# Attention bursts of a four-layer kernel: scores and values as one operation per query block, strips between eights, and a new order

## The chip, the cores and the metric

The kernel runs on one core of a Trainium2 chip. The metric is the time of one execution on the device in microseconds (us), as the median of several runs. The core has five engines with a queue of instructions each: TensorE (PE in the profile, with its weight loads as PEld), VectorE (DVE), ScalarE (ACT), GpSimd (POOL) and SyncE (SP, which here issues nearly all transfers). An engine works through its queue in order and waits at semaphores for the others.

## The reference

The input x has 2048 rows of 448 numbers (bf16). Four layers follow each other, each added to x: attention, gated MLP, attention, gated MLP, with the same weights in both rounds.

```
x = x + A(layernorm(x));  x = x + B(layernorm(x));  x = x + A(layernorm(x));  x = x + B(layernorm(x))

A: qkv = x @ wqkv, 16 heads of 28; row s attends to the rows s, s-2, s-4, ... s-14 (8 of them, those below 0 masked)
   o = softmax(q.k * 28**-0.5) @ v;  return o @ wo
B: return ((x @ w_gate) * (x @ w_up)) @ w_down      (448 -> 1792 -> 448)
```

## The kernel before

**Tiling.** Everything stays in on-chip memory; weights and x are loaded once. Layer norm is done by VectorE and ScalarE per block of 128 rows, and the result is transposed, by TensorE in the head and by transfers later. All large products (L349) are made as pairs: the contraction is cut into pieces of 64 rows, and two products of 64x128 tiles run side by side on the upper and lower half of the array. Such an operation is a "twin" (L652, L665): two outputs A and B, where the upper half works first on A and the lower on B, and then they cross over. At the crossing TensorE waits on its own semaphore until the other half's results are written.

**Attention.** The 2048 rows are cut into 17 query blocks (the first of 128, the others of 120 rows), taken as nine groups: block 0 alone, then pairs. For a group, `attn_front` (L812) makes the masked copies of q (`Qz`, L821, VectorE), the scores (L835, TensorE), the exponential in two halves (L844, ScalarE) and the minimum with a mask (L851, VectorE), also in halves. `attn_back` (L855) multiplies by the values (L869, TensorE), copies the result out of PSUM (L880, L884), and `norm` (L889) divides by the row sums (L894 to L907). Then `y_blocks` makes the out-projection.

The scores and values of a group are 64 small products each (32 for block 0, fewer and wider in the first layer's first six groups, `WIDE_S`). They use tiles of 64x32, eight of which work at once, and so stand as a burst between the whole products of 64x128. The scores of one group are one operation that takes four PSUM banks (`Banks(4)`). Its exponentials wait for all of them. The values of a group are one operation too, which waits for both halves of the exponentials and minima (L872).

**Strips.** A whole product can also be given as four strips of 64x32 (L351, recorded at L352), which use the burst's own tiles. A pair is then eight strips. An operation that lends its first steps as strips is the host of the burst.

**The order.** Operations are recorded in Python (`sc.add`) and get numbers. Which engine does an operation and in which order is a written list, `ORDER` (L102), and the PSUM banks come from another, `BANKS` (L163). An entry of TensorE's list such as `406*2/397` means: operation 406 (a burst), cut at k = 2 points, with the first two steps of 397 as strips at the cuts, and then the rest of 397. The cuts stand at equal shares (L242): 64 products become 21, 21 and 22 with two strip steps, four times 16 with three. At most three steps can be lent (`MAXALT`, L31), and only the first ones of a host. All waits of a burst and of its host are put ahead of the first of their instructions (L312 to L325).

Of the kernel before, what the change touches and what calls it, by code (L numbers as in the profile page):

```python
# [7 lines left out]
S = 2048  # L8
# [20 lines left out]
BURST = "C32"  # L29
WIDE_S = ((0, 0), (0, 1), (0, 2), (0, 3), (0, 4), (0, 5))  # L30
MAXALT = 3  # L31
# [63 lines left out]
def grp_nc(g):  # L95
# [21 lines left out]
    ),  # L117
    "act": (
# [12 lines left out]
    ),  # L131
    "dve": (
# [46 lines left out]
)  # L179


# [924 lines left out]
```

## Time and profile before

| | |
|---|---|
| Three runs | 387.46, 387.26, 386.85 us (median 387.26) |
| Span of the profiled execution | 386.8 us, the only time shown for it |
| Whole products (L349), 512 columns, for gate and up | 1146, 376 ns each as recorded |
| Products of the values (L869), 64 columns | 1024, 192 ns each as recorded |
| Products of the scores (L835), 64x32 tiles | 736, 191 or 199 ns each as recorded |
| Strips (L352) of WD, 448 columns | 216, 354 ns each as recorded |
| Weight loads (PEld) | 215.7 us busy, beside the products |

The granted clock of TensorE is 1.000 over the whole span. A product's recorded time holds its way through the array, and several are on their way at once, so the times of products can't be added: the distance between their starts tells what one costs. In the timeline a row is a run of equal products: start in us, time from the first's start to the last's end, engine, line, names, shapes and count. Because the ends overlap, the next row's start can stand ahead of the row's end.

### The profile page before, as it was taken

To read this page: it belongs to the slowest core of one execution; us is meant where nothing else is said; L and a number is where in the kernel's file an instruction comes from. 1 tells how busy PE (TensorE), PEld (TensorE's weight loads), DVE (VectorE), ACT (ScalarE), POOL (GpSimd) and SP (SyncE) were. 2 spreads that over 40 slices of the span, in tenths; PEclk is the share of its full clock that TensorE was granted. 3 is DMA by queue.
4 is the path that set the end of the run, shared out by engine and by line. 5 is a ranking of instruction groups with operands and counts; after the bars stand their busy time and mean duration, and the time that the engine had idled before them with its cause. 6 is when DMAs were issued, how large, how long until landed. Compare 5 with 4: busy or idle time off the path is not lost. (4 is left out here: it accounts for less than half of the span.)

```text
span 386.8 us, 14289 instructions
## 1 busy us (share of the span) xinstructions
PE 378.7 (98%) x6326; PEld 215.7 (56%) x6326; DVE 286.9 (74%) x644; ACT 204.3 (53%) x391; POOL 7.2 (2%) x33
## 2 busy tenths in 40 slices
PE   8999998999999999999999999999999999999997
PEld 3654576644554445555865666555555444445775
DVE  7988899998947887696776886578886887562423
ACT  5997886764516564364466426637653834143220
POOL 7000000000000000000000000000000000000000
PEclk9999999999999999999999999999999999999999
DMA  7665541801313041141104115400142005020004
GB/s 259 159 160 148 103 116 55 103 18 24 66 32 44 3 83 34 32 53 28 29 3 64 29 15 98 67 16 2 24 73 51 2 2 97 25 47 2 26 2 132
DMA packets 54881, 22.50 MB, mean 58 GB/s; under 512 B 45012, under 2 KB 54820, under 8 KB 54820
## 3 DMA queue, kind: packets, MB, share of 16 engines
q1 hardware_dynamic: 54676, 21.53, 27.5%
q8 instruction: 50, 0.82, 0.9%
q14 instruction: 11, 0.09, 0.1%
q10 hardware_dynamic: 144, 0.06, 0.1%
HBM read 8.54 MB, written 2.71 MB: 29 GB/s over the span
## 5 line engine op out<-in xcount | busy, mean ns | idle before, releaser
L349 PE MATMUL ps<-xnTb,WGU 64*128 64x512 bf16 (+1 forms) x1930 | 177.2, 333 | 0.9 <-issue 0.9
L349 PEld LDWEIGHTS ps<-xnTb,WGU 64*128 64x128 bf16 x1930 | 95.4, 94 | 73.2 <-issue 3.1
L960 ACT ACTIVATE g_sb<-ps 128x512 bf16<-128x512 f32 (+1 forms) x140 | 69.1, 511 | 91.3 <-PE ps L349 79.6
L963 DVE TENSOR_TENSOR hT<-g_sb,ps 128x512 bf16<-128x512 bf16 (+1 forms) x140 | 78.0, 574 | 39.9 <-ACT g_sb L960 36.7
L349 PE MATMUL ps<-WD,hT 64*128 64x448 bf16 x786 | 82.0, 349 | 0.1
L349 PEld LDWEIGHTS ps<-WD,hT 64*128 64x128 bf16 x786 | 38.9, 94 | 32.2 <-issue 1.0
L924 DVE TENSOR_TENSOR x_sb<-x_sb,ps 128x448 bf16<-128x448 bf16 x62 | 36.9, 614 | 26.1 <-PE ps L349 26.1
L349 PE MATMUL ps<-xnTa,WQK 64*128 64x512 bf16 (+1 forms) x486 | 52.2, 353 | 0.7 <-DVE xnTa L625 0.6
L844 ACT ACTIVATE E_sb<-ps,shift_sb 128x1024 bf16<-128x1024 f32 (+1 forms) x36 | 37.3, 1067 | 13.1 <-PE ps L835 13.1
L580 DVE BATCH_NORM_STATS2 st<-x_sb 128x6 f32<-128x448 bf16 x64 | 38.6, 615 | 1.5 <-DMA x_sb<-in_A_x_dram 1.2
L601 DVE TENSOR_SCALAR xn_sb<-x_sb,mv,rstd 128x896 bf16<-128x896 bf16 (+1 forms) x64 | 35.6, 573 | 4.4 <-ACT rstd L585 4.3
L349 PEld LDWEIGHTS ps<-xnTa,WQK 64*128 64x128 bf16 x486 | 23.3, 94 | 21.5 <-DVE WQK L527 0.7
L710 ACT ACTIVATE qk<-ps 128x1024 bf16<-128x1024 f32 (+1 forms) x29 | 26.2, 918 | 9.3 <-PE ps L349 9.2
L349 PE MATMUL ps<-wo_g,oT 64*128 64x448 bf16 x252 | 28.7, 349 | 0.2
L851 DVE TENSOR_TENSOR E_sb<-E_sb,MK 128x1024 bf16<-128x1024 bf16 (+1 forms) x36 | 23.3, 659 | 7.5 <-ACT E_sb L844 7.3
L895 ACT ACTIVATE R_sb<-R_sb 128x480 f32<-128x480 f32 (+1 forms) x34 | 20.4, 602 | 9.1 <-DVE R_sb L894 8.8
L907 DVE TENSOR_TENSOR oT<-O_sb,R_sb 128x480 bf16<-128x480 f32 (+3 forms) x36 | 22.0, 626 | 2.3 <-ACT R_sb L896 2.2
L349 PE MATMUL ps<-WV,xnTa 64*128 64x336 bf16 (+3 forms) x246 | 23.4, 304 | 0.1
L894 DVE STREAM_SHUFFLE R_sb<-O_sb 128x480 f32<-128x480 f32 (+1 forms) x34 | 23.2, 691 | 0.0
L583 ACT ACTIVATE lnv<-mv,eps_sb 128x2 f32<-128x2 f32 (+1 forms) x33 | 9.7, 292 | 22.7 <-DVE mv L582 22.6
L896 ACT ACTIVATE R_sb<-R_sb 128x480 f32<-128x480 f32 (+1 forms) x34 | 20.1, 601 | 0.4
L880 ACT ACTIVATE O_sb<-ps 128x512 f32<-128x512 f32 (+2 forms) x21 | 11.4, 567 | 12.9 <-PE ps L869 12.9
(65 smaller groups left out, 222.3 us busy)
## 6 DMA issues: line engine op xcount, KB each, us to landing
out_dram<-x_sb SPq DMA_DIRECT2D x15, 112.0 KB, 1.8
x_sb<-in_A_x_dram SPq DMA_DIRECT2D x3, 448.0 KB, 5.8
hT<-in_A_wqkv_dram SPq DMA_DIRECT2D x4, 224.0 KB, 4.5
WGU<-in_B_w_gate_dram SPq DMA_DIRECT2D x4, 224.0 KB, 3.5
WGU<-in_B_w_up_dram SPq DMA_DIRECT2D x4, 224.0 KB, 4.4
WD<-in_B_w_down_dram SPq DMA_DIRECT2D x2, 448.0 KB, 3.9
WGU<-in_B_w_gate_dram SPq DMA_DIRECT2D x2, 336.0 KB, 4.4
WGU<-in_B_w_up_dram SPq DMA_DIRECT2D x2, 336.0 KB, 4.5
```

The source lines that it names most:

```text
L349: return lambda E: E.matmul(out(), lhs(), rhs(), start=start, stop=stop)
L580: sc.add("dve", one(lambda E, B=B: E.bn_stats(st6[:, B, :], x_sb[:, B, :]), ("bn", li, B)), 525.0, deps=[("x", li - 1, B)] + ([("xn", li - ...
L601: sc.add("dve", one(lambda E, B=B, dst=dst, src=src: E.tensor_scalar(dst, src, mv[:, B, 0:1], rstd[:, B:B + 1], ALU.subtract, ALU.mult), ( ...
L710: return E.activation(dst, src, ACT.Copy) if hasattr(E, "activation") else E.tensor_copy(dst, src)
L844: return E.activation(E_sb[:, slot, 2 * hp:2 * hp + 2, 0:w], ps[:, b0:b0 + 2, 0:w], ACT.Exp, bias=shift_sb[:, 0:1], scale=SCALE)
L851: return E.tensor_tensor(e, e, MK[:, kind, 0:nc].unsqueeze(1).unsqueeze(1).to_broadcast([128, 2, w // nc, nc]), ALU.min)
L894: sc.add("dve", one(lambda E: E.stream_shuffle(R_sb[:, rs, 0:w], O_sb[:, os_, 0:w], [DH] * 32), ("Rs", li, qb)), dve_est(w) + 20.0, deps=[ ...
L895: sc.add("act", one(lambda E: E.activation(R_sb[:, rs, 0:w], R_sb[:, rs, 0:w], ACT.Ln), ("Rl", li, qb)), act_est(w, False), deps=[("Rs", l ...
L907: return E.tensor_tensor(oT[:, :, a % HALF:a % HALF + z - a], O[:, :, a - tok:z - tok], R_sb[:, rs, 0:w].rearrange("p (h n) -> p h n", h=4 ...
L924: sc.add("dve", one(lambda E: E.tensor_tensor(x_sb[:, B, :], x_sb[:, B, :], ps[:, bk[w], 0:D], ALU.add), ("x", li, B)), dve_est(D), deps=[ ...
L960: sc.add("act", one(lambda E, gs=gs, bk=bk: E.activation(g_sb[:, gs, 0:nt], ps[:, bk[0], 0:nt], ACT.Copy), ("G", li, j, fc)), act_est(nt), ...
L963: sc.add("dve", one(lambda E, gs=gs, bk=bk, fc=fc: E.tensor_tensor(hT[:, fc, hs, 0:nt], g_sb[:, gs, 0:nt], ps[:, bk[1], 0:nt], ALU.mult), ...
```

## The change

Scores and values are now two operations per group, one per half (for a pair of query blocks: one per block). Each half of the scores has a pair of PSUM banks of its own, and its exponential waits for that half alone. Each half of the values waits for its own half of the exponentials and for its own block's v. The copies out of PSUM wait for both.

Strips: every step of an operation can be lent, any number of steps, from any step on, and several hosts can share a burst: an entry such as `508/2/1` behind the star names the host, the number of steps and the first of them. The cuts are rounded to eight products (`cut_of`). An operation's waits are put ahead of its own first instruction, not ahead of the whole entry. `ORDER` and `BANKS` are new throughout: TensorE's products are the same in number and size but for strips (448 before, 400 after, the others back as whole products), and some copies out of PSUM change between ScalarE and VectorE.

```diff
-MAXALT = 3
...
-                    cut = [len(short) * (i + 1) // (k + 1) for i in range(k)] + [len(short)]
-                        if i < k:
-                            seq += [(host, fn) for fn in host.alt[i]]
-                    seq += [(host, n) for n in range(2 * k, len(host.ins))]
+                    hosts = [tuple(int(i) for i in (h + "/0").split("/")[:3]) for h in tail.split("+")]
+                    seq = [(self.ops[h], n, None) for h, k, f in hosts for n in range(2 * f)]
+                    sets = [[(self.ops[h], n, fn) for fn, n in self.ops[h].alt[f + i]] for h, k, f in hosts for i in range(k)]
+                    for i in range(len(sets) + 1):
+                        z = cut_of(len(short), i + 1, len(sets) + 1)
+                        seq += short[a:z] + (sets[i] if i < len(sets) else [])
...
+def cut_of(n, i, parts):
+    return n if i >= parts else min(n, (2 * n * i + 8 * parts) // (16 * parts) * 8)
...
-        bk = Banks(4, pair=True)
-        if li > 0 and g:
-            deps = deps + [("E", li, g - 1, 0), ("E", li, g - 1, 1)]
+        bks = [Banks(2, pair=True) for _ in range(2)]
...
+        for hp, ins in enumerate(parts):
+            ins[-1] = (ins[-1][0], [("Sh", li, g, hp)] + ([("S", li, qbs[hp])] if nd == 2 else [("S", li, qbs[0])] if hp else []))
+            first = sc.add("pe", ins, 0.0, deps=deps + [("Qz", li, g)], mode="C64" if wide else BURST, acquire=bks[hp], prio=prio, after=first)
...
-            sc.add("act", one(fe, ("Ex", li, g, hp)), act_est(2 * w), deps=[("S", li, qbs[-1]), prev, "c_shift"], release=[(bk, 2 * hp), (bk, 2 * hp + 1)], prio=prio)
+            sc.add("act", one(fe, ("Ex", li, g, hp)), act_est(2 * w), deps=[("Sh", li, g, hp), prev, "c_shift"], release=[(bks[hp], 0), (bks[hp], 1)], prio=prio)
...
-        sc.add("pe", ins, AV_EST * nd / 2, deps=[("E", li, g, 0), ("E", li, g, 1), "c_v"] + [(k, li, q) for k in ("V", "VT") for q in qbs] + [r[1] for r in oring], mode=BURST, acquire=bk, prio=prio)
+        for hp, ins in enumerate(parts):
+            ins[-1] = (ins[-1][0], [("Ah", li, g, hp)] + ([("AV", li, qbs[hp])] if nd == 2 else [("AV", li, qbs[0])] if hp else []))
+            first = sc.add("pe", ins, 0.0, deps=[("E", li, g, hp), "c_v"] + [(k, li, q) for k in ("V", "VT") for q in (qbs[hp:hp + 1] if nd == 2 else qbs)], mode=BURST,
+                           acquire=None if hp else bk, prio=prio, after=first)
...
-            sc.add(AVC_E, one(fo, ("Oc", li, g, c)), {"act": act_est(n), "dve": dve_est(n)}, deps=[("AV", li, qbs[0])] + [r[1] for r in oring],
+            sc.add(AVC_E, one(fo, ("Oc", li, g, c)), {"act": act_est(n), "dve": dve_est(n)}, deps=[("AV", li, qbs[-1])] + [r[1] for r in oring],
```

In the order that results, the bursts of 64x32 tiles stand as follows (products, with | for a strip step):

| | before | after |
|---|---|---|
| 32 without strips | 2 | 15 |
| 16 \| 16 | 0 | 3 |
| 64 without strips | 1 | 0 |
| 64 as 21 \| 21 \| 22 | 13 | 0 |
| 64 as 16 \| 16 \| 16 \| 16 | 6 | 5 |
| 64 as 24 \| 16 \| 24 | 0 | 3 |
| 64 as 40 \| 16 \| 8 or 8 \| 16 \| 40 | 0 | 4 |
| 64 as 16 \| 8 \| 16 \| 8 \| 16 | 0 | 2 |
| 96 (24 \| 24 \| 24 \| 24; 16 \| 16 \| 16 \| 48) | 1 | 1 |
| 128 (32 \| 32 \| 32 \| 32; none) | 2 | 1 |
| 64 values, then 64 scores as 16 \| 16 \| 16 \| 16 | 1 | 0 |
| 64 scores with seven steps in their first half, then 64 values | 0 | 1 |

The six bursts of wide scores (tiles of 64x64, first layer) are the same in both.

More of the change, by code (lines that the diff above doesn't have):

```diff
@@ L235, in schedule @@
                 w, _, tail = w.partition("*")
-                k, _, host = tail.partition("/")
                 got = [self.ops[int(i)] for i in w.split("+")]
-                seq = [(o, n) for o in got for n in range(len(o.ins))]
-                if k:
-                    short, k, host = seq, int(k), self.ops[int(host)]
-                    got.append(host)
-                    cut = [len(short) * (i + 1) // (k + 1) for i in range(k)] + [len(short)]
-                    seq, a = [], 0
-                    for i, z in enumerate(cut):
-                        seq += short[a:z]
+                seq = [(o, n, None) for o in got for n in range(len(o.ins))]
+                if tail:
+                    hosts = [tuple(int(i) for i in (h + "/0").split("/")[:3]) for h in tail.split("+")]
+                    short, a = seq, 0
+                    seq = [(self.ops[h], n, None) for h, k, f in hosts for n in range(2 * f)]
[3 more added lines that the diff above has]
+                        seq += short[a:z] + (sets[i] if i < len(sets) else [])
                         a = z
-                        if i < k:
-                            seq += [(host, fn) for fn in host.alt[i]]
-                    seq += [(host, n) for n in range(2 * k, len(host.ins))]
+                    for h, k, f in hosts:
+                        got.append(self.ops[h])
+                        seq += [(self.ops[h], n, None) for n in range(2 * (f + k), len(self.ops[h].ins))]
                 for o in got:
@@ L289, in emit @@
                     continue
-                for op, n in seq:
-                    if isinstance(n, int) and ((op.idx, n) in used or n == len(op.ins) - 1):
+                for op, n, _ in seq:
+                    if n is not None and ((op.idx, n) in used or n == len(op.ins) - 1):
                         count[e] += 1
@@ L311, in run @@
                 for got, seq in self.order[e]:
-                    waits = {}
-                    for op in got:
-                        for k in op.deps:
-                            src, n = self.ready[k]
+                    begun = set()
+                    for op, n, fn in seq:
+                        waits = {}
+                        for k in op.deps if op.idx not in begun else ():
+                            src, m = self.ready[k]
                             if src.dma is not None:
@@ L320, in run @@
                                     continue
-                                s, v = src.eng, value[(src.idx, n)]
+                                s, v = src.eng, value[(src.idx, m)]
                             waits[s] = max(waits.get(s, 0), v)
-                    for s, v in waits.items():
-                        if seen.get(s, 0) < v:
-                            E.wait_ge(sems[s], v)
-                            seen[s] = v
-                    for op, n in seq:
-                        if not isinstance(n, int):
-                            n(E)
-                            continue
-                        i = op.ins[n][0](E)
+                        begun.add(op.idx)
+                        for s, v in waits.items():
+                            if seen.get(s, 0) < v:
+                                E.wait_ge(sems[s], v)
+                                seen[s] = v
+                        i = (fn or op.ins[n][0])(E)
                         if op.dma is not None:
@@ L353, in pair, with alt_of @@
     ins = [(whole(*a[:5]), a[6]) for a in calls]
-    strips = [strip(*a[:6], c) for a in calls for c in range(0, 128, 32)] if all(a[6] is None for a in calls) else None
-    return ins, strips
-def alt_of(strips, keep=1):
-    n = 0
-    while n < len(strips) - keep and strips[n] is not None:
-        n += 1
-    return strips[:min(n, MAXALT)]
+    return ins, [(strip(*a[:6], c), w if c == 96 else None) for w, a in enumerate(calls) for c in range(0, 128, 32)]
+def alt_of(steps):
+    return [[(fn, None if w is None else 2 * i + w) for fn, w in step] for i, step in enumerate(steps)]
+def cut_of(n, i, parts):
+    return n if i >= parts else min(n, (2 * n * i + 8 * parts) // (16 * parts) * 8)
 def act_est(n, psum=True):
@@ L857, in attn_back @@
         nd = len(qbs)
-        bk = Banks(2, pair=True)
+        bk = Banks(2)
         while nd == 2 and rpos["o"] % NO == NO - 1:
@@ L861, in attn_back @@
         oring = [ring("o", ("N", li, q)) for q in qbs]
-        ins = []
+        parts = [[], []]
         for hc, d, c, b in [(hc, d, c, b) for hc in range(4) for d in range(nd) for c in range(2) for b in range(4)]:
@@ L868, in attn_back @@
             eo = (2 * eh + b % 2) * nc
[L869 removed]
+            parts[eb // 2].append((lambda E, b=b, c=c, o=o, vw=vw, eb=eb, eo=eo: E.matmul(ps[32 * b:32 * b + 32, bk[c], o:o + nc], vw, E_sb[64 * c:64 * c + 64, slot, eb, eo:eo + nc],
                                                                start=True, stop=True, tile_position=(64 * c, 32 * b)), None))
[L871 to L872 removed]
+        first = None
+        for hp, ins in enumerate(parts):
+            ins[-1] = (ins[-1][0], [("Ah", li, g, hp)] + ([("AV", li, qbs[hp])] if nd == 2 else [("AV", li, qbs[0])] if hp else []))
+            first = sc.add("pe", ins, 0.0, deps=[("E", li, g, hp), "c_v"] + [(k, li, q) for k in ("V", "VT") for q in (qbs[hp:hp + 1] if nd == 2 else qbs)], mode=BURST,
+                           acquire=None if hp else bk, prio=prio, after=first)
         o0, nq = oring[0][0], qb_info(qbs[0])[3]
```

14 lines of the change are left out of this document (5 added, 9 removed), and 127 rows, old and new, of tables (BANKS, ORDER).

## The prediction

> **What bounds the kernel now.** I read the page's busy times first, then the waits of TensorE, then the timeline of TensorE around each attention burst.
>
> ```profile
> span 386.8 us, 14289 instructions
> PE 378.7 (98%) x6326; PEld 215.7 (56%) x6326; DVE 286.9 (74%) x644; ACT 204.3 (53%) x391; POOL 7.2 (2%) x33
> ...
> 305.97 3.19 PE L349 MATMUL ps<-wo_g,oT 64*128 64x448 bf16 x32
> 309.00 15.27 PE L349 MATMUL ps<-xnTb,WGU 64*128 64x512 bf16 x140
> 324.11 1.49 PE L349 MATMUL ps<-WD,hT 64*128 64x448 bf16 x14
> ```
>
> TensorE is busy for 98% of the span; VectorE has the next share, 74%. The other engines matter only where TensorE waits for them. The last three rows give the pace. 32 products of 448 columns fill 305.97 to 309.00, and two run side by side on the two row halves, so a pair takes 3.03 / 16 = 0.189 us. 140 products of 512 columns fill 309.00 to 324.11, so a pair takes 15.11 / 70 = 0.216 us. Nothing can be saved there: the change removes no product and no column. What can move is the cost of the attention bursts and the waits.
>
> **What a burst costs.** The scores (L835) and values (L869) are small products on eight 64x32 tiles of the array. Between whole products (64x128 tiles, L349) they stand as bursts, with or without strips (L352): whole products cut into four, which run on the same eight tiles. Eight strips do the work of one pair, so I charge them the pair's time. A burst's cost is the time from its first small product to the next whole one, less its strips, plus the entry.
>
> Without strips, 32 products and 64:
>
> ```profile
> 152.25 0.75 PE L349 MATMUL ps<-WD,hT 64*128 64x448 bf16 x6
> 152.92 0.33 PE L835 MATMUL ps<-Qz,qk 64*32 64x80 bf16 x32
> 153.19 0.93 PE L349 MATMUL ps<-WD,hT 64*128 64x448 bf16 x8
> ```
>
> ```profile
> 52.41 0.68 PE L869 MATMUL ps<-E_sb,v_sb 64*32 64x64 bf16 x64
> 53.04 0.72 PE L349 MATMUL ps<-xnTb,WGU 64*128 64x256 bf16 x10
> ```
>
> Entry: three pairs from 152.25 end at 152.25 + 3 x 0.189 = 152.82, and the burst starts at 152.92: 0.10 us. So 32 products cost 0.27 + 0.10 = **0.37**, and 64 cost 0.63 + 0.10 = **0.73**.
>
> With strips: 64 scores as four times 16 around three steps, 64 values as 21, 21, 22 around two, 64 scores cut the same way, and 128 values as four times 32 around three steps:
>
> ```profile
> 158.77 0.26 PE L835 MATMUL ps<-Qz,qk 64*32 64x64 bf16 x16
> 158.84 0.38 PE L352 MATMUL ps<-WD,hT 64*32 64x448 bf16 x8
> ...
> 159.78 0.93 PE L349 MATMUL ps<-WD,hT 64*128 64x448 bf16 x8
> ```
>
> ```profile
> 84.08 0.27 PE L869 MATMUL ps<-E_sb,v_sb 64*32 64x64 bf16 x21
> 84.16 0.40 PE L352 MATMUL ps<-xnTb,WGU 64*32 64x512 bf16 x8
> ...
> 85.01 0.82 PE L349 MATMUL ps<-xnTb,WGU 64*128 64x512 bf16 x6
> ```
>
> ```profile
> 298.77 0.28 PE L835 MATMUL ps<-Qz,qk 64*32 64x64 bf16 x19
> ...
> 299.74 4.27 PE L349 MATMUL ps<-xnTb,WGU 64*128 64x512 bf16 x38
> ```
>
> ```profile
> 259.52 0.34 PE L869 MATMUL ps<-E_sb,v_sb 64*32 64x64 bf16 x32
> ...
> 261.30 0.39 PE L349 MATMUL ps<-xnTa,WQK 64*128 64x512 bf16 x2
> ```
>
> - 64 as 16s: 1.01 - 3 x 0.189 + 0.10 = **0.54**.
> - 64 by 21s: values 0.93 - 2 x 0.216 + 0.10 = **0.60**, scores 0.97 - 0.43 + 0.10 = **0.64**.
> - 128 as 32s: 1.78 - 3 x 0.216 + 0.10 = **1.23**.
>
> So a strip step is worth about 0.1 us when 16 products stand on each side of it, and two bursts of 32 cost 0.74, more than one burst of 64 with strips.
>
> **The sum of the bursts.** The six bursts of wide scores (64x64 tiles, first layer) are the same in both orders. The others now: values once 32 (0.37), once 64 (0.73), nine times 64 by 21s (5.40), once 96 by 24s (0.90, between 0.60 and 1.23), twice 128 (2.46), and once 64 with 64 scores by 16s behind it (1.27); scores six times by 16s (3.24), four times by 21s (2.56), once 32 (0.37). That is 17.3 us. In the new order, as the changed program issues it: 15 plain bursts of 32 (5.55); three of 32 as 16, 16 around one step (0.38 each, between 0.37 and 0.54: 1.14); five of 64 by 16s (2.70); three as 24, 16, 24 (between 0.54 and 0.64, I take 0.58 since only the middle one falls to 16: 1.74); four with a part of 40 beside 16 and 8 (between 0.60 and 0.73, I take 0.65: 2.60); one of 96 (0.90); two of 64 in five parts (0.54: 1.08); one of 128 values without strips (between 1.23 and 1.46, I take 1.27); one of 64 scores and 64 values with seven steps among the first scores (between 0.54 and 1.46, I take 1.15). That is 18.1 us, **+0.8 us**: the cut of a group into two operations gives 41 bursts where 32 stand now, and the smaller ones have no strips. With every open price at its low end the difference is -0.2, at its high end +2.5.
>
> The Trainium skill (TensorEngine Tiling, section Instruction Overhead) gives each product a fixed cost of about 60 cycles. At the 2.4 columns per ns of the pace rows that would be, as an estimate, 25 ns, hence 0.8 us for 32 products alone. The trace disagrees: 32 of them leave in 0.27 us. By the page bursts would cost by their products alone, the cut would be free, and the sum would be 0.8 lower.
>
> **The waits.**
>
> The first rows of TensorE in the view of waits, and one further on:
>
> ```profile
> PE ps L349 <- issue: 0.9, 1, 0.9
> PE ps L869 <- issue: 0.9, 1, 0.9
> ...
> PE ps L835 <- ACT E_sb L844: 0.3, 1, 0.3
> ```
>
> *Scores and values.* The group rows of the exponential and of the minimum, then a values burst that starts late:
>
> ```profile
> L844 ACT ACTIVATE E_sb<-ps,shift_sb 128x1024 bf16<-128x1024 f32 x32 | 34.5, 1108 | 12.3 <-PE ps L835 12.3
> L851 DVE TENSOR_TENSOR E_sb<-E_sb,MK 128x1024 bf16<-128x1024 bf16 x32 | 21.5, 686 | 7.5 <-ACT E_sb L844 7.3
> ```
>
> ```profile
> 62.44 0.60 PE L349 MATMUL ps<-WV,xnTa 64*128 64x336 bf16 x6
> 63.19 0.27 PE L869 MATMUL ps<-E_sb,v_sb 64*32 64x64 bf16 x21
> ```
>
> A score burst takes four PSUM banks, and once waited 0.3 us for the exponential to free them; with two pairs the first half needs only one pair. A values burst waits for both halves: two exponentials and a minimum, 2 x 1.11 + 0.69 = 2.9 us behind the last score; the first half alone is ready after 1.8. The burst at 63.19 is late: three pairs of 336 columns (0.142 each, the 448-column pace by its columns) end at 62.87, the entry makes 62.97, so 0.22 us are lost. Three others start late in the same way; I take 0.22 for each, an estimate. Together **-1.1 us** (0 if the new order puts the halves closer to their scores, which it does for two groups; -1.3 at best). What would then be late next is the normalisation of that group, which the out-projection needs; it has other groups' products in between. The change adds a wait per second half; behind it, on TensorE, stand that half's strips and the next whole products, which is why a half placed too early costs what it waits.
>
> *The crossing of row halves.*
>
> ```profile
> 37.04 1.93 PE L349 MATMUL ps<-wo_g,oT 64*128 64x448 bf16 x16
> 38.80 0.54 PE L349 MATMUL ps<-WV,xnTa 64*128 64x448 bf16 x4
> ```
>
> The 16 products from 37.04 need 8 x 0.189 = 1.51 but take 1.76: when one twin's second half follows its first at once, TensorE waits 0.25 for its own results. I count three such places now and two half-covered ones in the new order: **-0.5** (-0.75 to 0).
>
> *Issue.* The page's row of the queue that brings instructions:
>
> ```profile
> q8 instruction: 50, 0.82, 0.9%
> ```
>
> Twice TensorE stands for 0.9 us with nothing to wait for. Its 2 x 6326 = 12,652 instructions come in 50 packets of 0.82 MB / 50 = 16.4 kB, some 253 each, and a burst of 128 with its strips eats 304 in 1.78 us. Stretches where 256 instructions pass in under some 5 us are 16 in the old order and 10 in the new (from the burst prices and the paces), but two of the new ones are the densest of all. I take half a stall fewer, **-0.4** (-1.8 to +1.8). The Trainium skill (Runtime: NRT & Kernel Launch, section Instruction fetch mechanics) has TensorE's instructions refilled in blocks of 16 KiB, 256 each, a cost "mostly hidden". The size agrees with the 16.4 kB, the hiding not with the two stalls; by the page this term would be 0 and the sum 0.4 higher.
>
> *Everything else* was ordered anew: the head, the projections, which engine copies what. Nothing in the trace prices that. TensorE is idle for 386.8 - 378.7 = 8.1 us in all, so an order without fault gains a few us and one with twice the faults loses as much; I take 0 and keep -2 to +3 for the range.
>
> **Sum.** +0.8 - 1.1 - 0.5 - 0.4 = -1.2 us, against a span of 386.8: 385.6. The median of the runs shown, 387.26, stands 0.46 above that span, so the time would be **386.1 us**.
>
> **Rivals.**
> 1. *Nothing is left of it* (same). The waits go as said, but the bursts come out above the middle (+1.9 instead of +0.8), or the values wait again: 387.2 us. For it: the gains and the burst term are of one size, and a measurement of this kernel can tell about 0.2% from no change.
> 2. *VectorE takes over between 25 and 75 us* (slower). Busy time by stretch (TensorE, weight loads, VectorE, ScalarE), then two of the copies that move:
>
> ```profile
> 40.00:55.00 15.00, 14.53 (x380) 9.61 (x374) 14.07 (x33) 14.78 (x26) 0.00 (x0) 1.00 0.48 112
> 55.00:75.00 20.00, 18.93 (x476) 12.69 (x474) 18.92 (x48) 13.60 (x29) 0.00 (x0) 1.00 0.51 75
> ```
>
> ```profile
> L802 DVE CAST v_sb<-ps 128x672 bf16<-128x672 f32 x2 | 1.7, 853 | 0.0
> L710 DVE CAST qk<-ps 128x512 bf16<-128x512 f32 x1 | 0.7, 676 | 0.0
> ```
>
> Here VectorE (third number) is busy for 32.99 of 35 us, so 2.0 are free, and ScalarE is full in the first stretch (14.78 of 15). Until the fifth score group's minimum the new order gives VectorE one v copy, two qk copies and two short xnT copies more (0.85 + 1.35 + twice some 0.4 = 3.0 us, the last an estimate below the qk row) and takes two O copies away (some 0.6 each, between the two rows): some 1.8 more, 2.0 free. Against it: ScalarE is relieved by more than that. It decides from the point where those free 2.0 us can't be used, because they lie ahead of work that isn't ready; then each us is TensorE's loss, and the three gains above go with it: 387.26 + 1.8 + 0.8 = 389.9 us at most, 389.0 where half of the 1.8 tells.
> 3. *The refill of instructions* (slower). The 128 values in a row and the burst of 64 + 64 with seven strip steps each stall for 0.9, on top of the two stalls of now: +1.8 instead of -0.4, and 388.3 us. For it: one of two such bursts of now did stall; against it: the one at 259.52 did not.
>
> **Chances.** The forecast 0.47; rival 1 0.17; rival 2 0.20; rival 3 0.16. Faster by over 0.2% 0.47, within 0.17, slower 0.36. The range reaches from the forecast with the other waits also better by 2 and a little of the bursts (383.4) to rival 2 at its upper end (389.9).
>
> **What would show it.** The bursts: 41 of them, plain ones of 32 at 0.27 from first product to the next whole one, and their sum at 18 us. The values: no late start at their first halves, and no score burst that waits for the exponential. The crossing: no 0.25 in the out-projection pairs. Issue: its rows in the view of waits, now 1.8 us. Rival 2 would show as waits of TensorE for VectorE between 25 and 75 us, and VectorE over 95% there; rival 3 as "issue" at the two dense bursts. The prediction is wrong if the waits not named above grow by more than 1 us in the projections of the first 75 us, where TensorE loses most today.

## The result and the profile after

The changed kernel takes 390.47 us in the median of four runs (390.37 to 391.50), the kernel before 387.14 us (386.85 to 387.46): a ratio of **1.0083** (95% interval 1.0065 to 1.0101). The forecast was 386.1, faster.

The head of the page of the changed kernel, with the time of each engine:

```profile
span 388.7 us, 14171 instructions
PE 378.7 (97%) x6290; PEld 210.0 (54%) x6290; DVE 286.3 (74%) x651; ACT 200.5 (52%) x384; POOL 7.3 (2%) x33
```

TensorE is busy as long as before (378.7 us) and idle for 10.0 us instead of 8.1. So the 1.9 us between the two spans stand in the profile as idle time. From the view of waits, TensorE's rows (total, times, longest; a row named issue is a stall with nothing that the profile shows it to wait for):

```profile
PE ps L347 <- DMA xnTb<-xn_sb: 3.2, 4, 2.0
PE ps L509 <- DVE eps_sb L470: 1.3, 1, 1.3
PE ps L347 <- DVE mv L580: 0.7, 1, 0.7
PE ps L609 <- DVE xn_sb L599: 0.5, 1, 0.5
PE ps L613 <- DVE xn_sb L599: 0.5, 1, 0.5
...
PE ps L347 <- issue: 0.2, 1, 0.2
```

The first row has no counterpart before: the first product of a chunk (L347) waits for the transfers that transpose the layer norm's output (L602). The row put down to the mean and variance (L580) is of the same kind: it is the wait at 177.77, where the last transpose landed 0.09 us ahead of the product. Together that is 3.9 us as idle time. The stalls named issue went from 1.8 to 0.2 us, and no value burst starts late any more (entries of 0.09 to 0.15 us).

The longest wait in the timelines, first of TensorE, then of SyncE's queue:

```profile
47.63 0.64 PE L831 MATMUL ps<-Qz,qk 64*64 64x128 bf16 x32
50.28 1.92 PE L347 MATMUL ps<-xnTb,WGU 64*128 64x256 bf16 x32 [2.01 <-DMA xnTb<-xn_sb]
```

```profile
42.39 0.27 SPq L717 DMA_DIRECT2D vt<-qk  x1
42.70 0.60 SPq L440 DMA_DIRECT2D WGU<-in_B_w_gate_dram  x1
43.58 2.67 SPq L602 DMA_TRANSPOSE xnTb<-xn_sb  x2
46.30 0.82 SPq L717 DMA_DIRECT2D vt<-qk  x2
47.16 0.62 SPq L440 DMA_DIRECT2D WGU<-in_B_w_up_dram  x1
```

In the new order a store (vt) that waits for a copy of qk stands ahead of two loads of 336 KB. So one of the loads leaves at 42.70, right ahead of the two transposes. The same stretch before:

```profile
42.80 2.66 SPq L604 DMA_TRANSPOSE xnTb<-xn_sb  x2
45.51 4.49 SPq L719 DMA_DIRECT2D vt<-qk  x9
```

The two median rows from issue to landing, after and before (3.1 in the second profile of before):

```profile
xnTb<-xn_sb SPq DMA_TRANSPOSE x2, 5.4
```

```profile
xnTb<-xn_sb SPq DMA_TRANSPOSE x2, 3.9
```

The bursts came out near their prices. A plain one of 32, one with a part of 40, and the 128 values in a row:

```profile
54.21 0.32 PE L866 MATMUL ps<-E_sb,v_sb 64*32 64x64 bf16 x32
54.47 0.94 PE L347 MATMUL ps<-xnTb,WGU 64*128 64x256 bf16 x14
...
122.77 0.48 PE L831 MATMUL ps<-Qz,qk 64*32 64x64 bf16 x40
...
123.70 1.12 PE L347 MATMUL ps<-WD,hT 64*128 64x448 bf16 x10
...
295.36 1.40 PE L866 MATMUL ps<-E_sb,v_sb 64*32 64x64 bf16 x128
296.69 1.50 PE L347 MATMUL ps<-WD,hT 64*128 64x448 bf16 x14
```

0.26 + 0.10 = 0.36 us (priced 0.37); 0.93 - 2 x 0.189 + 0.10 = 0.65 (0.65); 1.33 + 0.10 = 1.43 (1.27). Added up in this way over the 35 narrow bursts: 18.6 us, forecast 18.1.

### The profile page after: what moved, and what is told of

The parts are those of the page before. It is cut to its first block, busy times and chain, and to the rows that moved or that the text cites. A ratio compares the mean times of both kernels' runs of the same rounds, so it can differ in the third digit from the quotient of the medians.

```text
span 388.7 us, 14171 instructions
## 1 busy us (share of the span) xinstructions
PE 378.7 (97%) x6290; PEld 210.0 (54%) x6290; DVE 286.3 (74%) x651; ACT 200.5 (52%) x384; POOL 7.3 (2%) x33
## 4 chain that ended last, share of the span: by engine, by line
PE 71%; DVE 5%; DMA 3%; ACT 1%; issue 0%; SPq 0%
PE ps L347 65%; DMA xnTb<-xn_sb 3%; PE ps L350 2%; PE ps L975 1%; PE ps L831 1%; DVE xn_sb L599 1%; PE ps L866 1%; DVE oT L907 1%; DVE hT L963 1%; DVE E_sb L848 1%; ACT g_sb L960 1%; DVE R_sb L894 1%; DVE x_sb L924 0%; DVE st L578 0%; DVE O_sb L880 0%
## 5 line engine op out<-in xcount | busy, mean ns | idle before, releaser
L347 PE MATMUL ps<-xnTb,WGU 64*128 64x512 bf16 (+1 forms) x1922 | 178.0, 333 | 3.4 <-DMA xnTb<-xn_sb 3.2
L347 PEld LDWEIGHTS ps<-xnTb,WGU 64*128 64x128 bf16 x1922 | 93.5, 94 | 76.8 <-issue 3.5
L347 PE MATMUL ps<-WD,hT 64*128 64x448 bf16 x796 | 82.8, 350 | 0.0
L347 PEld LDWEIGHTS ps<-WD,hT 64*128 64x128 bf16 x796 | 37.5, 94 | 33.1 <-DVE hT L963 0.3
L347 PE MATMUL ps<-xnTa,WQK 64*128 64x512 bf16 (+1 forms) x488 | 51.9, 353 | 1.0 <-DVE mv L580 0.7
L841 ACT ACTIVATE E_sb<-ps,shift_sb 128x1024 bf16<-128x1024 f32 (+1 forms) x36 | 37.4, 1068 | 18.6 <-PE ps L831 18.6
L578 DVE BATCH_NORM_STATS2 st<-x_sb 128x6 f32<-128x448 bf16 x64 | 37.8, 613 | 0.8 <-DMA x_sb<-in_A_x_dram 0.8
L599 DVE TENSOR_SCALAR xn_sb<-x_sb,mv,rstd 128x512 bf16<-128x512 bf16 (+1 forms) x64 | 35.6, 570 | 2.3 <-ACT rstd L583 2.1
L347 PEld LDWEIGHTS ps<-xnTa,WQK 64*128 64x128 bf16 x488 | 23.8, 94 | 21.2 <-DVE mv L580 1.2
L347 PE MATMUL ps<-wo_g,oT 64*128 64x448 bf16 x254 | 29.4, 350 | 0.0
L347 PE MATMUL ps<-WV,xnTa 64*128 64x336 bf16 (+3 forms) x252 | 23.3, 304 | 0.0
L880 ACT ACTIVATE O_sb<-ps 128x512 f32<-128x512 f32 (+2 forms) x23 | 12.3, 562 | 16.8 <-PE ps L866 16.5
```

Of the source, the lines that this page charges most:

```text
L347: return lambda E: E.matmul(out(), lhs(), rhs(), start=start, stop=stop)
L578: sc.add("dve", one(lambda E, B=B: E.bn_stats(st6[:, B, :], x_sb[:, B, :]), ("bn", li, B)), 525.0, deps=[("x", li - 1, B)] + ([("xn", li - ...
L599: sc.add("dve", one(lambda E, B=B, dst=dst, src=src: E.tensor_scalar(dst, src, mv[:, B, 0:1], rstd[:, B:B + 1], ALU.subtract, ALU.mult), ( ...
L841: return E.activation(E_sb[:, slot, 2 * hp:2 * hp + 2, 0:w], ps[:, b0:b0 + 2, 0:w], ACT.Exp, bias=shift_sb[:, 0:1], scale=SCALE)
```

## The experiments

All ratios are to the kernel before, run beside each version on the same chip. Line numbers in their profiles stand up to six above those of the changed kernel, since the written lists are longer. "Old order" is the order of the kernel before.

Four theories were tested. **O**: the loss is the new order, in which the first users of the DMA transposes stand too close behind them (O': because the layer norm's place on VectorE is late). **S**: the split of scores and values into halves, with waits and banks of their own, costs it. **V**: VectorE is the bound around 60 us, so time given back to TensorE there returns as a wait. **B**: the greater number of bursts costs it.

### The change in its three parts

**The cuts alone**: the kernel before, with one line changed.

```diff
-    cut = [len(short) * (i + 1) // (k + 1) for i in range(k)] + [len(short)]
+    n = len(short)
+    cut = [(2 * n * (i + 1) + 8 * (k + 1)) // (16 * (k + 1)) * 8 for i in range(k)] + [n]
```

> The kernel before, in which only the points are changed where a narrow product is cut by strips: multiples of eight (64 as 24, 16, 24) instead of equal parts (21, 21, 22). From the two traces: four score bursts go from 0.645 to 0.527 us and nine value bursts from 0.60 to about 0.52 us, 0.5 + 0.7 = 1.2 us, so 387.1 - 1.2 = 385.9 us (385.6 to 386.4). If the cost of a burst is hidden by what it makes wait, or the traced difference came from the other half's place and not from the cut: 387.1 us, no change.

Measured: **0.9933** (0.9914 to 0.9952), more than expected. A values burst of 64, from its first product to the next whole one:

```profile
83.24 0.28 PE L870 MATMUL ps<-E_sb,v_sb 64*32 64x64 bf16 x24
83.34 0.43 PE L353 MATMUL ps<-xnTb,WGU 64*32 64x512 bf16 x8
...
84.06 0.39 PE L350 MATMUL ps<-xnTb,WGU 64*128 64x512 bf16 x2
```

0.82 - 2 x 0.216 + 0.10 = 0.49 us, where 21, 21, 22 cost 0.60. Over all 13 such bursts the two traces differ by 1.5 us. The rest of the 2.6 us isn't priced; this trace has one issue stall of 0.5 us, where the two profiles of the kernel before have two.

**Cuts and halves in the old order**: the changed kernel's code; in its lists each operation has the place and banks of the kernel before, the two halves side by side.

```diff
 "pe": (
-  "... 254*2/498 ... 401 ..."        (before: values, scores)
+  "... 257+258*508/2 ... 409 410 ..."
```

> The changed kernel's code with the kernel before's order: scores and values in two halves with their own banks and waits, cuts at multiples of eight, but every operation at the place, in the burst and in the banks that it had before (both halves side by side). Theory O: the split itself costs nothing; 1.2 us for the cuts, and some 0.6 us for value bursts that no longer wait for the second half of the minimum, so 387.1 - 1.8 = 385.3 us (384.8 to 386.2). Theory S: the halves' own waits and releases cost, so 387.1 us or more, up to the changed kernel's 390.5 us. Theory V says nothing on it beyond theory O.

Measured: **0.9937** (0.9921 to 0.9953). The head of its page, and all of TensorE's waits:

```profile
span 384.1 us, 14280 instructions
PE 377.8 (98%) x6326; PEld 216.3 (56%) x6326; DVE 286.8 (75%) x644; ACT 204.0 (53%) x391; POOL 7.2 (2%) x33
```

```profile
PE ps L514 <- DVE hT L475: 1.8, 1, 1.8
PE ps L352 <- issue: 1.0, 1, 1.0
PE ps L352 <- DVE xnTa L628: 0.6, 1, 0.6
```

So the change comes apart into three: the cuts give -0.67%, the halves with their own banks and waits nothing that can be measured (0.9937 against 0.9933), and the **order searched anew costs +1.5%** (1.0083 against 0.9937), 5.7 us. The order stands here for the places of the operations, the banks, and the engines of some copies; these were not taken apart from each other. Theory S, that the split itself costs it, is refuted for halves that stand side by side; halves that stand apart are theory B's. Both of these versions beat both kernels.

**The kernel before, once more.**

> The kernel before, unchanged, as a second profile: its first profile had a span of 386.8 us, and two stalls named issue of 0.9 us each, at 67 and 290 us. If they belong to every execution, they are there again and the span is 386 to 387 us; if they come and go, one is missing and the span is nearer 385.5 us. The ratio is 1 by construction (within 0.002).

Measured: 0.9999 (0.9990 to 1.0007), span 386.2 at a time of 387.89 us: 1.7 us lie outside the span, as in the changed kernel (388.7 and 390.37). The issue stalls are there again, but 0.6 and 0.4 us long: their sizes change from execution to execution.

### The waits for the transposes

**Weights first**: the changed kernel, SyncE's list.

```diff
-  "... 89 370 90 307 305 368 369 91 372 ..."
+  "... 89 90 91 370 307 305 368 369 372 ..."      (90, 91: weight loads; 307, 305: transposes; 370: store)
```

> The changed kernel with one edit on SyncE alone: the last two loads of the gate and up weights stand ahead of the store that waits 10.6 us for a copy, as in the kernel before, instead of behind it. Theory O (the loss is the new order: first users of the DMA transposes stand too close behind them): these two loads sit right in front of the transposes that TensorE waits 2.0 us for at 50.3 us of the changed kernel's trace; with them gone from there, that wait and the 0.2 us for the weights at 56.6 us go, so 390.5 - 2.2 = 388.3 us (388.0 to 389.2). Theory S (the split of the narrow products into halves, with 41 bursts in place of 32, costs it): no order on SyncE bears on that, 390.5 us. Theory V (VectorE is the bound between 40 and 55 us): the wait passes from the transposes to VectorE's copies and products there, under 0.7 us won, 389.8 us or more.

Measured: **1.0073** (1.0045 to 1.0100), so nothing sure, and theory O fell in this form. The wait did shrink, and others grew:

```profile
49.05 3.21 PE L352 MATMUL ps<-xnTb,WGU 64*128 64x256 bf16 x55 [0.77 <-DMA xnTb<-xn_sb]
...
77.91 1.25 PE L352 MATMUL ps<-xnTb,WGU 64*128 64x512 bf16 x10 [0.60 <-DMA xnTb<-xn_sb]
...
177.59 0.82 PE L352 MATMUL ps<-xnTa,WQK 64*128 64x512 bf16 x6 [1.06 <-DVE hT L968]
```

At 50 us 1.24 us were won: the two transposes landed 4.0 us after their issue in the median row, not 5.4. At 78 and 178 us, where the changed kernel waits 0.18 and 0.69 us by the same view, 0.8 us of them went again, and 0.4 us to a longer issue stall (0.6 us, where the changed kernel has 0.2).

**The reverse**: the old-order version, with SyncE's list there made as in the changed kernel.

```diff
-  "... 89 90 91 96 305 307 ..."                  (370 further on)
+  "... 89 370 90 305 307 91 96 ..."
```

> The version with the old order (0.9937), in which SyncE's order around the first DMA transposes of the gate and up products is made as in the changed kernel: the store that waits for a copy ahead of the last two weight loads, one of these right ahead of the two transposes and one behind. In the changed kernel the transposes landed 5.5 us after their issue there, and 2.9 us without. Theory O: TensorE, which has no room there in the old order either (48.6 us landed, 48.9 us used), waits 2 us, and nothing takes it back: 0.9937 + 0.005 = 0.9985 to 0.9995. Theory V (TensorE's time before 78 us is not the bound, as taking the wait away gave 0.001): 0.9937 to 0.996.

Measured: **1.0018** (1.0002 to 1.0034) against 0.9937: 3.1 us for this one edit, as much as theory O had and more, but for the most part by another way than the load. SyncE's queue, in the old-order version and then here:

```profile
42.65 2.69 SPq L607 DMA_TRANSPOSE xnTb<-xn_sb  x2
```

```profile
44.60 0.27 SPq L722 DMA_DIRECT2D vt<-qk  x1
44.92 0.60 SPq L445 DMA_DIRECT2D WGU<-in_B_w_gate_dram  x1
45.57 3.79 SPq L607 DMA_TRANSPOSE xnTb<-xn_sb  x2
```

In the old order the copy that the store waits for comes later: the store leaves at 44.60 (at 42.39 in the changed kernel), and the transposes behind it, whose inputs were ready by then, leave 2.9 us later than without the edit. The last one lands at 51.08. So this run shows what a waiting store does to the queue behind it; what the load alone costs can't be told from it. TensorE, and its granted clock (the number ahead of the last two) by stretches:

```profile
51.38 3.84 PE L352 MATMUL ps<-xnTb,WGU 64*128 64x256 bf16 x42 [2.38 <-DMA xnTb<-xn_sb]
```

```profile
50.00:51.50 1.50, 0.12 (x2) 0.15 (x4) 1.07 (x3) 0.66 (x1) 0.00 (x0) 0.77 0.60 92
51.50:52.50 1.00, 1.00 (x12) 0.81 (x11) 0.00 (x0) 0.00 (x0) 0.00 (x0) 0.50 0.92 297
52.50:53.50 1.00, 1.00 (x14) 0.81 (x12) 0.02 (x1) 0.44 (x2) 0.00 (x0) 0.50 1.12 229
53.50:54.50 1.00, 1.00 (x15) 0.89 (x13) 1.00 (x3) 1.00 (x2) 0.00 (x0) 0.63 0.66 208
```

The wait of 2.4 us costs itself, and in this execution the clock stood at 0.50 for some 3.4 us (from the four rows), of which 2.9 us lie behind the wait: 1.4 us more. In six of the twelve executions the mean clock was 0.995 or 0.996; their median is 389.2 us, that of the other six 387.6. The Trainium skill (TensorE: Matmul & The Clock Gate, Part 1: The HAM clock gate) has the clock halved after an idle window of about 3.4 us that runs freely. Here an idle time of 2.4 us was enough, and in half of the executions, if the others waited as long as the profiled one; of the changed kernel's four executions, with the wait of 2.0 us in the profile, one has 0.996 too (391.50 us).

**All sites**: weights first, and small moves at five other waits. On SyncE two transposes are swapped, and a store (the expectation calls it a weight load) is put behind three transposes; on TensorE one independent product goes ahead of each waiting one at 178, 218 and 246 us.

```diff
 "sp"  -  "673 677 675"   "445 597 451 449 447"
       +  "673 675 677"   "445 451 449 447 597"
 "pe"  -  "918 881"   "1061 965"   "1231 1162"
       +  "881 918"   "965 1061"   "1162 1231"
```

> The run above, with small moves at the five other places where TensorE waited for transposes: two transposes swapped on SyncE for 111 us, one weight load put behind the transposes for 78 us, and on TensorE one independent product moved ahead of the waiting one at 178, 218 and 246 us. Theory O: besides the 2.2 us of the run above, the waits of 0.35, 0.83, 0.85, 0.50 and 0.14 us go (2.7 us), so 390.5 - 4.9 = 385.6 us (385.0 to 387.0), below the kernel before. Theory S: these waits were slack that the bursts would take in any case, so at most half of it is seen, 388 us or more. Theory V: VectorE writes the inputs of these transposes, and moving their users only moves the wait: 389 us or more.

Measured: **1.0011** (0.9999 to 1.0023), 2.8 us better than the changed kernel and less than expected. The waits at 178 and 218 us are gone and stay gone (at 179.48 the product stands behind the other without a gap); at 246 us the burst moved ahead starts some 0.25 us late instead; those at 78 and 111 us are there still. The profiled execution is the slowest of the twelve (390.05 us); it waits 1.3 us at 50.6 us, once more ahead of the first products that read the transposes, though the view names E_sb, and has 1.2 us of issue stalls.

```profile
176.67 2.97 PE L352 MATMUL ps<-xnTb,WGU 64*128 64x512 bf16 x26
179.48 0.81 PE L352 MATMUL ps<-xnTa,WQK 64*128 64x512 bf16 x6
```

### VectorE's share

Four more statistics instructions in the layer norm of the chunk that is used at 78 us, written to unused memory, in both orders (the new one with the weights first); and, as a counter-test in the new one, the four there cut to 32 columns, which leaves out most of that variance.

```diff
+  more = [(lambda E, B=B: E.bn_stats(st6[:, 16 + B, :], x_sb[:, B, :]), None)] if (li, j) == (1, 1) else []
-  sc.add("dve", one(lambda E, B=B: E.bn_stats(st6[:, B, :], x_sb[:, B, :]), ("bn", li, B)), ...
+  sc.add("dve", more + one(lambda E, B=B: E.bn_stats(st6[:, B, :], x_sb[:, B, :]), ("bn", li, B)), ...
(less:)  x_sb[:, B, 0:32 if (li, j) == (1, 1) else D]
```

> The changed kernel with the weights ahead (1.0073), and four more statistics instructions on VectorE (0.6 us each, 2.3 us in all), each just ahead of one that the second chunk's layer norm needs, around 62 to 68 us. Theory V (in the new order VectorE's queue up to the layer norm sets when TensorE gets its transposed input at 78 us): nothing covers them, the wait there grows from 0.77 us by about 2.3 us and the time by some 2 us, to a ratio of 1.012 to 1.014. Theory O alone (only the place of users and transposes matters, VectorE has slack): the wait grows by under 0.5 us, 1.0073 to 1.0085.

> The four more statistics instructions of the run before last (2.3 us on VectorE), in the version with the kernel before's order (0.9937). There the same transposes landed at 75.6 us, 1.9 us ahead of their first user at 77.5 us. Theory V (VectorE is the bound there in any order): 2 us more, 0.999. Theory O (the old order keeps room between the transposes and their users, which is what the new one lacks): at most 0.4 us of it is not covered, plus what TensorE waits for VectorE's other results, in all 0.5 to 1 us, 0.995 to 0.9963.

> The same kernel (1.0073), in which the four statistics instructions of the second chunk's layer norm read 32 columns and not 448, so that this part of the variance is left out; VectorE is some 1.8 us earlier there. Theory V: the transposes land about 1.5 us earlier, the wait of 0.77 us at 78 us is gone and the next one at 110 us is no longer; 1.0053 to 1.006. Theory O alone: no change, 1.0073, with the wait at 78 us still there.

Measured: new order **1.0120** (1.0107 to 1.0133) against 1.0073, old order **0.9980** (0.9969 to 0.9992) against 0.9937: 1.8 us and 1.7 us for four instructions of 0.61 us each, 2.4 us. With less work 1.0064 (1.0050 to 1.0078), no sure gain, though VectorE's busy time from 55 to 75 us fell to 18.0 us there. Around 60 us time added to VectorE is paid for the most part, in either order; time taken away isn't won. That is half of theory V's mechanism, and it isn't what divides the two kernels: the old order is as sensitive. The stretch from 55 to 75 us (VectorE is the third busy time), in the changed kernel and then in the old-order version:

```profile
55.00:75.00 20.00, 19.86 (x484) 12.93 (x480) 19.66 (x50) 14.68 (x33) 0.00 (x0) 1.00 0.53 125
```

```profile
55.00:75.00 20.00, 19.01 (x478) 13.00 (x476) 18.99 (x49) 13.77 (x29) 0.00 (x0) 1.00 0.49 89
```

### The layer norm earlier

Statistics, the two ScalarE steps and the normalisation up to four places earlier in their engines' lists, for six chunks with the transposes up to three places earlier on SyncE, and then for three chunks with SyncE's list left alone (on top of the version with all sites). Moves stop where an input would be passed.

> The changed kernel with the weights ahead (1.0073), in which, for the six chunks whose transposes TensorE waited for, the layer norm's steps on VectorE and ScalarE stand up to four places earlier in their engine's order and the transposes up to three on SyncE, as far as their inputs allow; TensorE's order is untouched. Theory O' (the new order puts the layer norms too late on VectorE, although VectorE has the time): the transposes land 2 to 3 us earlier, the waits of 0.77, 0.55, 1.22, 0.75 and 0.14 us go, less some 0.5 us for products of VectorE that are put behind: 1.0073 - 0.0075 = 1.000 (0.999 to 1.002). Theory V (VectorE has no time to give, so the time returns as waits on what was put behind): 1.006 to 1.009, with the same sum of waits under other names.

> The version with small moves at all sites (1.0011 of the kernel before; its trace still waits 0.94, 0.89 and 0.25 us for transposes at 79, 112 and 338 us), with the layer norm's steps of these three chunks up to four places earlier in VectorE's and ScalarE's order, and nothing moved on SyncE: in the run with everything earlier the layer norm's transposes stood ahead of the value transposes on SyncE, and TensorE waited 12.5 us for those. Theory O' (the place on VectorE): the three waits go, 2.1 us less, a ratio of 0.9957 (0.995 to 0.998). Theory V (VectorE has no time to give before 78 us): only those at 112 and 338 us can go, and what was put behind is waited for instead: 0.999 to 1.004.

Measured: **1.0853** (1.0835 to 1.0872) and **1.0247** (1.0224 to 1.0271). Both went far past what either theory had. In the first the transposes stood ahead of those of the values in SyncE's queue and waited there for their inputs:

```profile
PE ps L871 <- DMA v_sb<-vt: 12.5, 3, 7.4
PE ps L352 <- DVE hT L968: 5.4, 6, 2.6
```

In the second the waits for the transposes are gone, and TensorE waits for what VectorE now does later:

```profile
72.33 0.93 PE L352 MATMUL ps<-WD,hT 64*128 64x448 bf16 x8 [2.63 <-DVE hT L968]
```

So these shifts of places cost more than the waits that they were to take away; whether another order of VectorE would give the transposes earlier isn't shown.

### The number of bursts

**Halves apart**, in the old order: thirteen bursts of 64 taken apart.

```diff
-  "257+258*508/2"     (13 such)
+  "257*508/1 258"
```

> The version with the kernel before's order (0.9937), with thirteen bursts, score and value, each taken apart into its halves as the changed kernel does it: the first half of 32 products by one strip step as 16, 16 (0.34 us), the second as 32 in one piece (0.37 us) behind the strips' host, where 24, 16, 24 took 0.51 us; 45 bursts and not 32. Theory B (each burst more costs its traced price): 13 x 0.19 = 2.5 us, 0.9937 + 0.0064 = 1.000 (0.999 to 1.0015). If bursts hide in waits, or the earlier half's earlier exponentials give it back: 0.9937 to 0.9955.

Measured: **1.0142** (1.0127 to 1.0158) against 0.9937: 7.9 us, three times the traced price. TensorE's busy time rose by 4.4 us (382.2 against 377.8) and its idle time by 2.9. The second half ends later, and the copies, divisions and projections behind it with it; waits for them that the version before did not have:

```profile
PE ps L352 <- DVE oT L912: 0.7, 2, 0.4
...
PE ps L355 <- ACT g_sb L965: 0.5, 1, 0.5
PE ps L352 <- DVE O_sb L889: 0.4, 1, 0.4
```

**Fewer bursts**, in the new order: halves joined, ten groups in the first run, only the seven adjacent ones in the second (36 and 39 bursts are left, not the 31 and 34 of the expectations, since the four with a part of 40 and the 128 values in a row were one burst each already).

```diff
-  "637 638*503/2"   "542 353 543"             (ten groups; 542 353 543 is not adjacent)
+  "637+638*503/2"   "542+543*353/2/2"
```

> The version with small moves at all sites (1.0011 of the kernel before), with ten pairs of neighbouring halves of a score or value product put back side by side and cut together by strips, so that 31 bursts are left of 41. Theory B (the number of bursts costs part of the loss): by the traced bursts, two plain halves of 0.36 us become one of 0.51 us, and pieces cut 40, 16, 8 (0.65 to 0.78 us) become 24, 16, 24 (0.53 us); with four plain halves in a row of 1.42 us against 0.8 us for six short pieces, some 2.3 us in all, so a ratio of 0.9952 (0.994 to 0.997), about 386.1 us where the kernel before is 387.95 us. If the bursts are covered by waits that end last anyway: 1.0011, no change. If the later start of a half delays its exponentials and minimum: above 1.0011.

> The version with small moves at all sites (1.0011), with only those seven groups of halves joined that stand next to each other in TensorE's order: pieces cut 40, 16, 8 or 16, 16 and 32 become 24, 16, 24, and four plain halves in a row become six pieces; 34 bursts in place of 41, and no half more than 1 us later. By the traced bursts 0.85 us (the traces of the fewer-bursts run) to 1.4 us (the plain prices) less. Theory B (bursts cost their traced price, and the other run lost by what it moved far): 0.9975 to 0.999. If joining delays what waits for the first half, as in the run with fewer bursts: above 1.0011.

Measured: **1.0110** (1.0096 to 1.0125) and **1.0045** (1.0023 to 1.0067), both worse than the 1.0011 that they started from. So theory B, by which fewer bursts should win, fails here; that the joined halves delay what waits for them, or that denser code stalls, is read from single profiles alone. Rows of the first of the two:

```profile
PE ps L352 <- issue: 1.6, 2, 1.4
PE ps L836 <- ACT E_sb L846: 1.3, 1, 1.3
```

The second has the same 1.6 us of issue in its profile, and its runs spread over 5 us (387.41 to 392.50). In both the waits for transposes are longer too: 3.2 and 2.4 us in the view, 1.5 in the version that they started from.

**Shorter pieces**, in the old order.

```diff
-  "789+790+805+806*863/3"   "1167+1168+1191+1192*1313/3"   "1347+1348+1371+1372*1280/3"
+  "789+790+805+806*863/5"   "1167+1168+1191+1192*1313/4"   "1347+1348+1371+1372*1280/7"
```

> The version with the old order (0.9937), with its three longest bursts cut finer: 128 value products into eight pieces of 16 in place of four of 32 (1.23 us), 96 into six of 16 in place of four of 24 (0.90 us), and 128 into five pieces in place of four (1.23 us). By the traced prices (64 in four pieces of 16: 0.50 us, so 128 in eight about 1.0 us and 96 in six about 0.75 us) 0.5 us less: 0.9925 (0.9915 to 0.9935). If the strips cost more than they save: 0.9937 to 0.995.

Measured: **0.9995** (0.9986 to 1.0005), 2.2 us worse where 0.5 better was expected. Right behind the 128 values in five pieces:

```profile
259.80 0.32 PE L871 MATMUL ps<-E_sb,v_sb 64*32 64x64 bf16 x24
260.05 0.61 PE L352 MATMUL ps<-xnTb,WGU 64*128 64x512 bf16 x4
261.96 1.25 PE L352 MATMUL ps<-xnTb,WGU 64*128 64x512 bf16 x10 [1.30 <-issue]
```

The finer cuts put 56 strips in the place of 14 whole products, and TensorE then stands for 1.3 us with nothing shown that it waits for. The version that it started from has one such stall, of 1.0 us, at 66.7 us.

## Why the prediction was wrong

- **The bursts, +0.8: near.** 18.6 us measured, 18.1 forecast; for the kernel before 17.6 by the same count, without the issue stall that stands in one of its bursts, where the forecast had 17.3. Two prices were low: 128 values in a row 1.43 (1.27), 64 and 64 with seven steps 1.43 (1.15; 1.30 in the run with the weights first). The sum hid two parts: the cuts are a gain (1.5 us in the traces, 0.67% in time), and the 41 bursts of the new order use it up again (the same code needs 16.6 us of bursts in the old order).
- **Halves, -1.1: the late starts went as forecast, but the halves alone don't do it.** (0.3 and four times 0.22 add up to 1.2.) In the new order no narrow burst starts late. In the old order, with the same halves, the score burst's wait is gone, but the values at 44, 52 and 63 us still start 0.24, 0.30 and 0.21 us behind the products ahead, where 0.10 is the entry (0.25, 0.23 and 0.32 before); the fourth late start (209 us) is missing in the second profile of before already. A burst with halves in sequence costs some 0.025 us more, and in time halves alone changed nothing (0.9937 against 0.9933).
- **The crossing, -0.5: right in the trace** (three waits of 0.23 to 0.30 us before, one of 0.07 after). **Issue, -0.4: open.** 1.8 and 1.0 us in two profiles of before and 0.2 after would fit, but two versions with the same bursts have 0.9 and 1.2. Rival 3 did not happen at the two bursts named. That a dense stretch can be followed by a stall is shown by the shorter pieces; that the refill of instructions is its cause is not.
- **"Everything else was ordered anew ... I take 0": this step failed.** The order by itself costs 1.5%. The prediction counted waits of before that go and priced none that a new order could make. In the traces the changed kernel takes 4.6 us longer than the old-order version (spans of 388.7 and 384.1 us). By the distances of the starts it waits 4.9 us for DMA transposes (2.0 us at 50 us, the rest at 78, 111, 178, 218, 246 and 338 us; 3.9 us of it stand in the view), where the view of the old order has no such row. Its bursts cost 2.0 us more, and the old order's stall of 1.0 us, late starts and crossings count the other way. The prediction's own sign came: a wait that it had not named, of 2.0 us, within the first 75 us. Both lists were at hand; the store ahead of the weight loads could have been read from SyncE's.
- **Rival 2** named VectorE between 25 and 75 us. VectorE is over 95% busy from 55 us on, as it said (19.66 of 20 us), and added time is dear there (1.8 us for 2.4), but in both orders, and the waits of the changed kernel there are for transposes, with VectorE's names on few. Its 389.9 was near the time for a reason that is at most a part.
- **From span to time** the prediction added 0.46; it is 1.6 to 1.8 in every run whose span is on record. By that the profiled execution of before took some 388.5 us, an estimate, 1.4 above the median; so the 1.9 us between the two profiles stand for 3.3 us of time.

What is shown of the 5.7 us of the order by experiment: five small moves and the weights give back 2.8, most of it with no wait left at 178 and 218 us. What the other 2.9 us divide into stays open. The bursts are 2.0 us longer in the trace, and by the distances of the starts 2.1 us of waits for transposes are left at 79, 112 and 338 us, but the attempts to take them away on VectorE's side moved more time than they saved.

## What to carry to other kernels

Take a change that brings its own order apart first: the new code in the old order, and each part alone. Here that turned a loss of 0.8% into a gain of 0.6% at once. In a tightly packed order a place can't be priced by what stands at it: time added at one place was paid for the most part or several times over, a wait taken away often came back at the next place, so an order must be judged by measuring it whole. Before forecasting, read each queue of the new order for what stands ahead of transfers that TensorE needs next, and for what that itself waits for.

## What the runs showed of the hardware

- Two transposes right behind a load of 336 KB landed 5.4 us after their issue in the median row, 4.0 in the same order without it; in the old order behind such a load 3.8, where their issue took 3.79 us and not 2.69.
- TensorE's granted clock fell to 0.50 for some 3.4 us, 2.9 of them behind an idle time of 2.4 us; the mean clock tells of the same in half of the executions.
- 64 small products around two strip steps cost 0.49 us as 24, 16, 24 and 0.60 as 21, 21, 22.
- Stalls of TensorE named issue differ between executions of the same kernel (0.9 and 0.9, then 0.6 and 0.4 us); one of 1.3 us stands behind a dense stretch of small instructions.
